# Routed attention and a cosine router with eight experts: an earlier transpose of the last batch's first logits, and one more GpSimd drain near the end

## The chip, the cores and the metric

The kernel runs on one NeuronCore of a Trainium2 chip. The metric is the device time of one execution in microseconds (us), as the median of several runs. TensorE is called PE here and in the profile, VectorE DVE, ScalarE ACT, GpSimd POOL and SyncE SP; SP issues most DMAs, and POOL those whose rows are picked by an index (gathers and scatters).

## The reference, cut to what matters

Attention comes first: 4 batches, 8 heads, 768 tokens, 64 wide. Queries and keys are assigned to the nearest of 16 centroids of their head, and a query attends only to the keys of its own cluster. The heads of a token, side by side, are a row x of 512 numbers. A router then picks one of 8 experts for every one of the 3072 rows, and the expert's two layers are applied:

```python
mask = q_assign[:, :, :, None] == k_assign[:, :, None, :]
attn = softmax(where(mask, q @ k.T / 8, -1e9));  x = rows(attn @ v)   # (3072, 512)
logits = unit(x) @ unit(expert_emb).T / tau                           # (3072, 8)
expert_idx = argmax(logits, axis=1)
gate_w = softmax(logits)[arange(N), expert_idx]
for e in range(8):
    mask = expert_idx == e
    out[mask] = gate_w[mask, None] * (relu(x[mask] @ w1[e]) @ w2[e])
```

## The kernel before, in words

Every engine executes its instructions in the order in which the program writes them: the whole kernel stands under a manual schedule for all five engines. What an instruction needs from another engine it waits for at its place, and what stands behind it on its own engine waits with it.

**Attention.** The loop over `units` goes through 16 pairs (a batch and two heads), each in two halves of the queries and six groups of keys. `scores` multiplies on PE, `expo` takes the exponential on ACT, `attend` multiplies with v on PE and lets DVE add up the weights in `acc`. For each half (`g`) `total` sums `acc` over the partitions with PE and takes the reciprocal on DVE (line 562), `divide` makes the finished x, turned, in `xT` (line 589, DVE), and `rows` turns it back on DVE (line 606) and stores it by DMA from SP in `x_rows` (line 613).

**Routing of a batch** (`route_pieces`). `products` multiplies `xT` with the experts' unit rows on PE into a bank of PSUM from `misc` (line 632); `misc` has two banks, taken in turns. `logits` is one transpose on DVE out of that bank into the tile `lt` (line 644). `read` loads the rows x again from `x_rows` for `norms`, which ACT takes. `choose` finds the best expert on DVE and counts on POOL. For the last batch the halves come apart: `products(0)` is issued in the last turn of the attention loop, directly behind that loop's last `rows`, and `products(1)` and `logits(1)` come after the last `divide`.

**Gates.** `gate_pieces(0, B - 1)` holds four steps for the first three batches: `gates[0]` a root on ACT, `gates[1]` three DVE instructions, `gates[2]` an exponential on ACT, `gates[3]` four DVE instructions (lines 710 to 716) and four small DMAs from SP to `gate_rows`.

**Experts.** `Places` computes for every token its place in the list of its expert. The rows of an expert are worked off in items. Four `early` items of 128 rows (`E0`) are filled from the first batches. Sixteen `later` items follow: eight `sized` ones of 272 down to 160 rows ("wide items"), and eight `block` ones of 128, by turns, the last being a block. An item has its expert's `w1` and `w2` loaded by SP into one of two slots (2 MB each), its rows fetched by gathers from POOL (`fetch`), turned (`turn_x`), multiplied with `w1` (`hidden`, line 1261, or `sized_hidden`, line 1176), passed through a relu on ACT, multiplied with `w2` (`result`, line 1277, or `sized_result`, line 1213), weighted by the gates and scattered to `out` by POOL (line 1052). `result` issues one scatter of 128 rows itself. A wide item's scatters, one for each 128 pieces of a quarter row, are issued by `send` one item later; the last wide item, of 160 rows, has five, and they come in the turn of the last block (`i == LAST`) ahead of its own `hidden`.

At the very end the framework adds (line 1633): SP waits for the semaphores of all DMAs, each engine executes a drain, and all engines meet at a barrier.

Of the kernel before, what the change touches and what calls it, by code (L numbers as in the profile page):

```python
# [39 lines left out]
def kernel(  # L40
# [12 lines left out]
    nc = tc.nc  # L53
# [637 lines left out]
    def gate_pieces(b0, b1):  # L691

        n = NJ * (b1 - b0)
        own = slice(NJ * b0, NJ * b1)
        lg, sq = lg_all[:, own], sq_all[:, own]

        def root():
            nc.scalar.activation(sq, sq, ACTF.Sqrt)

        def gate_scale():  # L700
            nc.vector.tensor_scalar(sq, sq, 1e-6, None, ALU.add)
            nc.vector.reciprocal(sq, sq)
            nc.vector.tensor_tensor(lg, lg, bc(sq, [P, n, E], 2), ALU.mult)

        def gate_exp():
            nc.scalar.activation(lg, lg, ACTF.Exp)

        def gate_sum():
            gate = gate_p[:, own]
            nc.vector.tensor_reduce(gate, lg, axis=AXX, op=ALU.add)  # L710
            nc.vector.tensor_scalar(gate, gate, 1e-9, None, ALU.add)
            nc.vector.reciprocal(gate, gate)

            if b0 > 0:
                return
            nc.vector.transpose(gate_t, gate_p)
            to = gate_rows[S * b0 : S * b1].rearrange("(j g t) o -> g j (t o)", g=NQ, t=SQ)
            for g in range(NQ):
                nc.sync.dma_start(out=to[g], in_=gate_t[SQ * g : SQ * g + n])

        return root, gate_scale, gate_exp, gate_sum
# [328 lines left out]
    def scatter(to, at, of, n):  # L1050

        inst = nc.gpsimd.indirect_dma_start(  # L1052
            out=to,
            out_offset=bass.IndirectOffsetOnAxis(ap=at, axis=0),
            in_=of,
            in_offset=None,
            bounds_check=n - 1,
            oob_is_err=False,
        ).ins
        tc.declare_no_dep(  # L1060
            inst, group="out", reason="a row of out is written by one slot of one item"
        )
        tc.add_to_no_dep_group("out", inst)
# [16 lines left out]
    def weights1(it, parts=1):  # L1080
        it.e = expert_of(it)
        for i in range(parts):
            load_part(w1s[it.slot], moe_w1, it.e, KD, i, parts)

    def weights2(it, parts=1):
        for i in range(parts):
            load_part(w2s[it.slot], moe_w2, it.e, KF, i, parts)
# [35 lines left out]
    def order_x(it):  # L1123

        d = mo[it]
        d["rows"] = xip.tile([P, KD, NQ, SQ], F32, tag="rows", name="rows")
        nc.gpsimd.tensor_copy(d["rows"], d["xin"].rearrange("p w (c i) -> p c w i", i=SQ))
# [29 lines left out]
    def order_w2(it):  # L1157

        w2 = mo[it]["w2"] = szp.tile([P, KF, DM], F32, tag="w2o", name="w2o", bufs=1)
        for f in range(KF):  # L1160
            nc.vector.tensor_copy(
                w2[:, f].rearrange("p (g w i) -> p g w i", w=NQ, i=SQ),
                w2s[it.slot][:, f].rearrange("p (w g i) -> p g w i", w=NQ, i=SQ),
            )
# [75 lines left out]
    def send(it):  # L1240

        u0 = FIRST[it.j]
        for u in range(WIDE[it.j]):
            at = flat(spidx)[:, u0 + u : u0 + u + 1]
            scatter(out_pieces, at, mo[it]["ys"][:, u], NQ * N)
        del mo[it]

    def flat(t):
        return t.rearrange("p k w -> p (k w)")

    def hidden(it, halves=(0, 1)):

        d = mo[it]
        for half in halves:
            if half == 0:
                d["hT"] = mop.tile([P, F], F32, tag="hT", name="hT")
            f0 = 512 * half
            bk = psH.tile([P, 512], F32, tag="h_ps", name="h_ps")
            for m in range(0, 512, P):
                for c in range(KD):  # L1260
                    nc.tensor.matmul(  # L1261
                        bk[:, m : m + P],
                        lhsT=w1s[it.slot][:, c, f0 + m : f0 + m + P],
                        rhs=d["xT"][:, P * c : P * c + P],
                        start=(c == 0),
                        stop=(c == KD - 1),
                    )
            nc.scalar.activation(d["hT"][:, f0 : f0 + 512], bk, ACTF.Relu)  # L1268
# [133 lines left out]
    with tc.manual_schedule(engines=by_hand):  # L1402
# [49 lines left out]
        products, logits, read, norms, choose = route[B - 1]  # L1452
        pb = Places(1, rtb)
        gates = gate_pieces(0, B - 1)
        gates[0]()
        hidden(E0[0], (0,))
        order_x(E0[3])
        total(ngroups - 1)
# [7 lines left out]
        hidden(E0[0], (1,))  # L1466
        gates[3]()
        weights1(E0[2])
        logits(0)
        read(0, NJ, P - SQ, P)  # L1470
        products(1)
        hidden(E0[1], (0,))
# [48 lines left out]
        def overflow():  # L1521
            n_used = nc.values_load(used[0:1, 0:1], min_val=0, max_val=KX + NO)
            slot = later[-1].slot

            def more(j0, n):
                for j in range(j0, j0 + n):
                    it = Item("whole", KX + j, slot, more_tables)
                    it.col, it.gates, it.xin = j, more_gates, xin
                    weights1(it)
                    weights2(it)  # L1530
                    fetch(it)
                    order_x(it)
                    turn_x(it, nc.scalar.copy)
                    hidden(it)
                    result(it)

            with tc.If(n_used > KX):  # L1537
                more_tables = [None] + [
                    mop.tile([P, NO], I32, tag=f"more{i}", name=f"more{i}", bufs=1)
                    for i in range(2)  # L1540
                ]
                xin = szp.tile([P, max(WIDE), P], F32, tag="ys", name="ys")[:, 0:NQ]
                pb.hot_blocks(NB, NO)
                pb.tokens(NO)
                pb.token_rows(more_tables[1], more_tables[2])
                more_gates = mop.tile([P, NO], F32, tag="more_gates", name="more_gates", bufs=1)
                pb.hot_gates(NO)
                pb.gates(more_gates)
                more(0, MORE[0])
                with tc.If(n_used > KX + MORE[0]):  # L1550
                    more(MORE[0], MORE[1])
                    with tc.If(n_used > KX + MORE[0] + MORE[1]):
                        more(MORE[0] + MORE[1], MORE[2])

        LAST = len(later) - 1
        for i, it in enumerate(later):
            if i == LAST - 1:
                overflow()
                weights1(later[LAST])
                weights2(later[LAST])  # L1560
            if it.kind == "sized":
                order_w2(it)
            if i + 1 < len(later):
                turn_x(later[i + 1])
            if i > 0 and i + 2 < len(later) and later[i + 2].kind == "sized":
                fetch(later[i + 2])
            if i > 0 and later[i - 1].kind == "sized":
                send(later[i - 1])
            if it.kind == "sized":
                sized_hidden(it)  # L1570
            else:
                hidden(it)
            if i == 0:
                pb.gates(slot_gates)
            for j in range(i + 2, min(i + 4, len(later))):
                if later[j].kind == "block" and later[j] not in mo:
                    if it.kind == "sized":
                        nc.gpsimd.tensor_copy(pace, mo[it]["hT"][0:1, KF - 1, 0:1])
                        fetch(later[j])
            if i + 2 < LAST:  # L1580
                weights1(later[i + 2])
                if it.kind == "sized":
                    weights2(later[i + 2])
            if it.kind == "sized":
                sized_result(it)
            else:
                result(it)
            if i == 0:
                fetch(later[2])
                spread_gates()  # L1590
            if i + 2 < LAST and it.kind != "sized":
                weights2(later[i + 2])
# [45 lines left out]
```

## Time and profile before

| | |
|---|---|
| time, median of 3 runs | 716.82 us (714.88 to 720.92) |
| own time of the profiled execution | 709.36 us |
| its span, first to last instruction | 707.6 us |
| granted PE clock, mean of the span | 0.995 |
| busy: PE, DVE, ACT, POOL | 690.8, 382.6, 265.1, 264.2 us |
| transpose of `logits` at 344.34, DVE | 0.24 us |
| gate arithmetic on DVE around it | 342.19 to 344.41 |
| the last wide item's scatters, POOL | 687.44 to 693.52 |
| the last block's scatter, POOL | 700.93 to 701.90 |
| closing drain of POOL | 6.02 us, from 700.7 |

A profile is one execution. Its times count from the first instruction. A row of a timeline gives start, duration, engine, line, operation, output and inputs, and in brackets the idle time of the engine before it with what ended that. PEld is the loading of weights into PE, which goes on beside the matmuls. An engine's name with a q (POOLq, SPq) is its instruction queue: drains, semaphore waits and the issuing of DMAs are counted there and not as busy time. In a table by stretches each row has the stretch, its length, the busy time and number of instructions of PE, PEld, DVE, ACT and POOL, then the granted PE clock (1.00 is full), the share of the DMA engines and GB/s.

### The profile page before, as it was taken

The page shows a single profiled execution, that of the slowest core. Times are in us where ns is not written, and L with a number is a line of the kernel's source. Part 1 is how long each engine was busy: PE and PEld are TensorE (multiplying, and loading weights), DVE is VectorE, ACT ScalarE, POOL GpSimd, SP SyncE. Part 2 cuts the span into 40 slices and gives each one's busy share as a digit, 9 for nine tenths or more (in the row PEclk, how much of TensorE's full clock was granted, in tenths as well). Part 3 has the DMA queues.
Part 4 walks back from the last instruction along what each step waited for, and adds up shares of the span by engine and source line. Part 5 has one row for each costly group of instructions (what it writes and reads, how often), then busy time and mean ns, then how long its engine had stood idle before and what let it go on. Part 6 is the DMA issues. An engine that isn't in the chain of part 4 may idle for free.

```text
span 707.6 us, 16122 instructions
## 1 busy us (share of the span) xinstructions
PE 690.8 (98%) x6518; PEld 456.2 (64%) x6518; DVE 382.6 (54%) x665; ACT 265.1 (37%) x446; POOL 264.2 (37%) x402
## 2 busy tenths in 40 slices
PE   6999999999999999999899999999999999999995
PEld 3444444444444444455876668897979797979793
DVE  4788888989889999989483121340220303031210
ACT  4566665677566755676215110101010111111110
POOL 2122222322224222353213546736264554544412
PEclk9999999999999999999999999999999999999999
DMA  9536665886657678879798987268668686869450
GB/s 150 91 60 110 105 104 87 153 159 108 100 108 146 120 146 152 183 190 329 184 278 305 342 314 268 81 233 287 258 226 299 198 310 226 320 242 330 142 192 28
DMA packets 244124, 135.55 MB, mean 192 GB/s; under 512 B 207808, under 2 KB 207810, under 8 KB 244044
## 3 DMA queue, kind: packets, MB, share of 16 engines
q1 hardware_dynamic: 237852, 121.28, 64.0%
q0 software_dynamic: 6016, 13.12, 5.4%
q8 instruction: 54, 0.88, 0.5%
q14 instruction: 26, 0.21, 0.1%
q10 hardware_dynamic: 176, 0.05, 0.0%
HBM read 115.92 MB, written 13.12 MB: 182 GB/s over the span
## 4 chain that ended last, share of the span: by engine, by line
PE 79%; DVE 6%; DMA 5%; issue 5%; POOL 1%; SPq 1%; ACT 1%; POOLq 0%; DVEq 0%; ACTq 0%
PE s_ps L484 18%; PE o_ps L506 15%; PE y_ps L1277 10%; PE h_ps L1261 9%; PE h_ps L1176 9%; PE y_ps L1213 5%; PE misc L1213 5%; DMA out_dram<-ys,spidx 3%; PE x_ps L1176 3%; DVE acc L525 2%; DMA x_rows<-xb 2%; PE misc L396 2%; PE misc L553 2%; PE misc L632 1%; SPq L613 1%
## 5 line engine op out<-in xcount | busy, mean ns | idle before, releaser
L495 ACT ACTIVATE prob<-s_ps 128x768 f32<-128x768 f32 x192 | 153.7, 812 | 95.2 <-PE s_ps L484 82.1
L484 PE MATMUL s_ps<-qT,kT 64*64 64x384 f32 x1536 | 156.0, 482 | 0.0
L506 PE MATMUL o_ps<-prob,v 64*64 64x385 f32 x1536 | 142.0, 486 | 0.0
L525 DVE TENSOR_TENSOR acc<-acc,prob 128x768 f32<-128x768 f32 x128 | 125.6, 982 | 8.8 <-ACT cd L422 0.5
L506 PEld LDWEIGHTS o_ps<-prob,v 64*64 64x64 f32 x1536 | 54.6, 133 | 70.3 <-issue 58.5
L1261 PE MATMUL h_ps<-xTm,w1s 128*128 128x128 f32 x768 | 90.0, 278 | 0.0
L1261 PEld LDWEIGHTS h_ps<-xTm,w1s 128*128 128x128 f32 x768 | 89.0, 195 | 1.4 <-issue 1.0
L1222 DVE STREAM_TRANSPOSE ys<-y_ps 128x256 f32<-128x256 f32 (+4 forms) x16 | 6.7, 417 | 153.4 <-PE y_ps L1213 153.4
L539 POOL TENSOR_TENSOR o_sum<-o_sb 128x385 f32<-128x385 f32 x30 | 32.0, 1067 | 146.3 <-ACT o_sb L530 146.3
L1052 POOL DMA_INDIRECT out_dram<-ys,spidx x56 | 56.7, 1013 | 74.7 <-DVE ys L1236 59.8
L1277 PE MATMUL y_ps<-w2s,hT 128*128 128x512 f32 x192 | 84.5, 593 | 0.0
L484 PEld LDWEIGHTS s_ps<-qT,kT 64*64 64x64 f32 x1536 | 56.0, 133 | 38.1 <-issue 34.9
L1176 PE MATMUL h_ps<-xTs,w1s 128*128 128x272 f32 (+7 forms) x384 | 72.9, 346 | 1.1 <-ACTq L1537 1.1
L1176 PEld LDWEIGHTS h_ps<-xTs,w1s 128*128 128x128 f32 x384 | 66.6, 190 | 8.0 <-issue 2.4
L1268 ACT ACTIVATE hT<-h_ps 128x512 f32<-128x512 f32 x24 | 14.3, 596 | 148.1 <-PE h_ps L1261 148.1
L484 PE MATMUL s_ps<-hot 64*64 64x384 bf16 x768 | 64.7, 325 | 2.2 <-ACT prob L495 1.1
L1041 POOL DMA_INDIRECT xs<-x_rows,gpidx x56 | 57.3, 1023 | 17.1 <-issue 16.8
L574 POOL COPY inv<-inv 32x12 f32<-32x12 f32 x120 | 43.0, 358 | 54.6 <-DVE inv L571 50.2
L1277 PEld LDWEIGHTS y_ps<-w2s,hT 128*128 128x128 f32 x192 | 35.6, 190 | 40.2 <-issue 40.2
L484 PEld LDWEIGHTS <-hot 64*64 64x64 bf16 x768 | 23.6, 106 | 39.4 <-issue 38.1
L1213 PE MATMUL y_ps<-hTs,w2o 128*128 128x272 f32 (+7 forms) x256 | 48.0, 346 | 0.0
L1213 PE MATMUL misc<-hTs,w2o 128*128 128x272 f32 (+7 forms) x256 | 48.0, 346 | 0.0
(264 smaller groups left out, 679.5 us busy)
## 6 DMA issues: line engine op xcount, KB each, us to landing
w1s<-in_moe_w_dram SPq DMA_DIRECT2D x18, 2048.0 KB, 10.6
w2s<-in_moe_w_dram SPq DMA_DIRECT2D x18, 2048.0 KB, 13.3
v<-in_v_dram SPq DMA_DIRECT2D x128, 48.0 KB, 2.1
q<-in_q_dram SPq DMA_DIRECT2D x60, 96.0 KB, 3.4
k<-in_k_dram SPq DMA_DIRECT2D x60, 96.0 KB, 3.6
x_rows<-xb SPq DMA_DIRECT2D x60, 96.0 KB, 2.8
xr<-x_rows SPq DMA_DIRECT2D x9, 512.0 KB, 4.0
w1s<-in_moe_w_dram SPq DMA_DIRECT2D x4, 1024.0 KB, 9.9
```

The lines of the kernel that those rows point to most:

```text
L484: nc.tensor.matmul(s_ps[D * half : D * half + D, h, 0:HS], lhsT=l[rows, half], rhs=r[rows], start=part == (1 if len(parts) < 2 else 0), st ...
L495: nc.scalar.activation(d["prob"][:, :, 0:HS], d["s_ps"][:, :, 0:HS], ACTF.Exp, scale=scale)
L506: nc.tensor.matmul(g["o_ps"][D * h : D * h + D, half, 0:HE], lhsT=ld[n]["v"][keys, j, h], rhs=d["prob"][keys, h, 0:HE], start=(j == 0), st ...
L525: nc.vector.tensor_tensor(g["acc"], g["acc"], d["prob"][:, :, 0:HS], ALU.add)
L539: add(t["o_sum"][:, hq], t["o_sb"][:, 0], t["o_sb"][:, 1], ALU.add)
L574: nc.gpsimd.tensor_copy(inv2[M * to : M * to + M, :, i % 2], inv[M * i : M * i + M])
L1041: nc.gpsimd.indirect_dma_start(out=to, out_offset=None, in_=of, in_offset=bass.IndirectOffsetOnAxis(ap=at, axis=0), bounds_check=n - 1, oo ...
L1052: inst = nc.gpsimd.indirect_dma_start(out=to, out_offset=bass.IndirectOffsetOnAxis(ap=at, axis=0), in_=of, in_offset=None, bounds_check=n - 1,
L1176: nc.tensor.matmul(bk, lhsT=w1s[it.slot][:, c, P * f : P * f + P], rhs=d["xT"][:, c, 0:C], start=(c == 0), stop=(c == KD - 1),)
L1213: nc.tensor.matmul(bks[g][:, 0:C], lhsT=d["w2"][:, f, P * g : P * g + P], rhs=d["hT"][:, f, 0:C], start=(f == 0), stop=(f == KF - 1),)
L1261: nc.tensor.matmul(bk[:, m : m + P], lhsT=w1s[it.slot][:, c, f0 + m : f0 + m + P], rhs=d["xT"][:, P * c : P * c + P], start=(c == 0), stop ...
L1277: nc.tensor.matmul(bk, lhsT=d["hT"][:, P * c : P * c + P], rhs=w2s[it.slot][:, c], start=(c == 0), stop=(c == KF - 1),)
```

## The change

The call `logits(0)`, the transpose of the first half of the last batch's logits, moves from behind `gates[3]` and the load of an expert's `w1` to directly behind `gates[0]`, ahead of the last half's `total`. In the turn of the last item, a drain instruction of POOL is added behind the scatters that `send` issues.

```diff
         pb = Places(1, rtb)
         gates = gate_pieces(0, B - 1)
         gates[0]()
+        logits(0)
         hidden(E0[0], (0,))
         order_x(E0[3])
         total(ngroups - 1)
...
         hidden(E0[0], (1,))
         gates[3]()
         weights1(E0[2])
-        logits(0)
         read(0, NJ, P - SQ, P)
         products(1)
         hidden(E0[1], (0,))
...
             if i > 0 and later[i - 1].kind == "sized":
                 send(later[i - 1])
+                if i == LAST:
+                    nc.gpsimd.drain()
             if it.kind == "sized":
                 sized_hidden(it)
```

## Prediction

> **What bounds the kernel now.** I read the page first, its busy rows and clock row, then the chain of work that ended last, then the timelines of the two stages that the diff touches.
>
> ```profile
> PE 690.8 (98%) x6518; PEld 456.2 (64%) x6518; DVE 382.6 (54%) x665; ACT 265.1 (37%) x446; POOL 264.2 (37%) x402
> PEclk9999999999999999999999999999999999999999
> ```
>
> TensorE (PE) is busy for 98% of the span, so there is little to win but in its few holes, in stretches where it is busy but slow, and in what lies behind its last matmul. The digits of PEclk are too coarse to show a short drop of the clock; a table by stretches is needed for that. The chain of waits around the end of attention (start, duration, what):
>
> ```profile
> 343.90 0.28 DVE gate_p L712
> 344.18 0.02 issue
> 344.20 0.21 DVE gate_t L716
> 344.41 0.18 DVE lt L644
> 344.59 0.04 issue
> 344.63 0.87 PE misc L632 x32
> 345.50 5.40 PE h_ps L1261 x32
> 350.90 0.44 PE x_ps L1152 x4
> 351.34 3.57 PE h_ps L1261 x32
> ```
>
> Two things stand here. The path runs over VectorE (DVE): `products(1)` (L632) waits for `logits(0)` (L644), which stands in DVE's order behind the gate arithmetic. And two equal halves of an expert, 32 matmuls each, take 5.40 and 3.57 us. From 355 us on the chain is PE without a hole up to the last item, but for the branch around 667 us. The timelines of PE and DVE say what else was ready:
>
> ```profile
> 332.96 0.87 PE L632 MATMUL misc<-xT,embT 128*32 128x96 f32 x32
> 338.81 3.74 PE L1261 MATMUL h_ps<-xTm,w1s 128*128 128x128 f32 x32
> 344.63 0.87 PE L632 MATMUL misc<-xT,embT 128*32 128x96 f32 x32 [2.08 <-DVE lt L644]
> ...
> 335.88 0.57 DVE L606 STREAM_TRANSPOSE xb<-xT 128x384 f32<-128x384 f32 x1
> 338.44 2.56 DVE L562 RECIPROCAL den<-misc 128x384 f32<-128x384 f32 x1 [1.99 <-PE misc L553]
> 341.03 0.62 DVE L589 SCALAR_TENSOR_TENSOR xT<-o_sum,den 128x384 f32<-128x384 f32 x1
> ```
>
> PE sits idle from 342.55 (338.81 + 3.74) to 344.63. What `logits(0)` reads was ready at 333.83, and the other input of `products(1)`, xT of L589, at 341.65. The clock by stretches (PEclk is the third column from the right):
>
> ```profile
> 342.41:345.82 3.41, 1.32 (x37) 1.04 (x36) 1.90 (x8) 0.81 (x2) 0.00 (x0) 1.00 0.40 59
> 345.82:349.24 3.42, 3.42 (x18) 3.42 (x18) 1.15 (x7) 0.00 (x0) 1.18 (x6) 0.50 0.36 82
> 349.24:352.65 3.41, 3.41 (x33) 3.41 (x32) 0.00 (x0) 1.07 (x2) 2.70 (x3) 1.00 1.01 390
> ```
>
> After a stretch of 3.41 us in which PE was busy for 1.32, the next 3.42 us were granted half the clock: 18 matmuls where the following stretch has 33. That is the 5.40.
>
> The end of the span: two rows of GpSimd's (POOL's) timeline, two of the last line, L1633 (duration min/median/max in ns, first and last start), and one of SyncE's waits (total, times, longest):
>
> ```profile
> 692.55 0.97 POOL L1052 DMA_INDIRECT out_dram<-ys,spidx  x1 [0.30 <-issue]
> 700.93 0.97 POOL L1052 DMA_INDIRECT out_dram<-y,sidx  x1 [7.41 <-ACT y L1288]
> ...
> L1633 SPq EVENT_SEMAPHORE  x13: 17/28/25632, 678.0 to 707.5; - x13
> L1633 POOLq DRAIN  x3: 40/113/6017, 700.7 to 707.3; - x3
> ...
> SPq L1633 <- PEq L1633: 3.1, 2, 2.6
> ```
>
> SyncE's long wait runs from 677.95 for 25.63 us, to 703.58: the landing of the last scatter. POOL's closing drain starts at 700.70 and takes 6.02 us, to 706.72, 3.14 us beyond that landing. SyncE has finished its own list at 704.32 and waits 2.6 us at the barrier; POOL is what comes last there.
>
> **Part A, the transpose of `logits(0)` moved forward.** It is one DVE instruction (L644, 0.24 us at 344.34) and no DMA. It is moved past DVE's reciprocal, divide, row transpose and seven gate instructions; no instruction of another queue changes place.
>
> At its new place it stands behind the row transpose that ends at 336.45. Its input has been ready for 2.6 us, so it waits for nothing. Queued behind it is the reciprocal (L562), for which DVE idles 1.99 us anyway, until PE's row sums at 338.4. The 0.24 us fall into that hole: cost nothing. If `products(0)` were later than 338.2, each us would hold the reciprocal, the divide and `products(1)`; it is 4.4 us away from that.
>
> At its old place it goes. `products(1)` then waits for xT (341.65) and for PE's own queue (342.55): PE is what is late next, so the whole hole of 2.08 us closes, less some 0.05 for the semaphore. The `misc` bank into which it writes was freed by `logits(0)` itself, at 336.7.
>
> With the hole goes the half clock. By the starts, L1261 of E0[1]'s first half took 350.74 - 345.43 = 5.31 us; its second half, at full clock, 354.75 - 351.17 = 3.58. That is 1.73 us more. Part A: 2.03 + 1.73 = **3.8 us**.
>
> [...]
>
> Does the 3.8 us survive? PE meets no wait from 355 to 650 us. Most weight loads are released by PE and move with it. One is not: w1 of E0[2], issued by SyncE at 346.90 behind the gate rows, lands at 355.0. PE wants it at 361.97, then at 358.2: 3.2 us of room. The gate gathers (first issue 349.34, median 5.3 us to landing) are in by about 356.5, the first of them by 355; the first eviction that reads one moves from 362.01 to 358.2. `choose` and the counts move forward about 1.2 us (DVE does `logits(1)` at 344.41 instead of 345.57) and the ranks on PE, then at 351.0, need them at about 347.5. The rank arithmetic on DVE (355.1 to 371.7) hangs on PE and shifts with it.
>
> **Part B, the drain behind the last wide item's five scatters.** Before it stand those scatters: the last issued at 692.55, landed some 2.2 us later (median of these issues in the last 22 us), at about 694.75. Behind it on POOL stands one thing, the last block's scatter, whose y is ready at 700.66. No other engine waits for POOL. So the cover is 5.9 us from that landing.
>
> The trace has no drain in mid-kernel. From below: a drain with nothing outstanding takes 0.04 to 0.11 us, by the same row. From above: the closing drain's remainder, 3.14 us beyond a landing. The latter is nearest, since scatters are outstanding here too: 694.75 + 3.14 = 697.9, hidden with 2.8 us to spare. [...]
>
> What it brings depends on what those 3.14 us are. The transfers of that stretch (703.58 to 706.72) are one packet:
>
> ```profile
> DMA packets 1, 0.01 MB, mean 3 GB/s; under 512 B 0, under 2 KB 0, under 8 KB 0
> q14 instruction: 1, 0.01, 0.7%
> ```
>
> No data move; 8 KB of instructions are fetched. Either the drain settles all transfers since the start of the kernel one by one, or it fetches code that 700 us of other work pushed out. In both cases an early drain pays in the idle 5.9 us, and the closing one has one scatter to settle: it ends near 703.58 + 0.5 at most. Then SyncE, at 704.32, is late next. Behind the barrier come 0.88 us (706.72 to 707.6), so the span would end at 705.2: 2.4 us less. The lower end is 0 (the 3.14 us are paid by each drain), the upper 2.4, since SyncE's list stays. I take **2.4**: drains with nothing to settle are short, so the cost is not that of any drain.
>
> **Sum.** 3.8 + 2.4 = 6.2 us. The profiled execution has a span of 707.6 and its own time of 709.36; they become 701.4 and 703.2. It lies 7.5 us under the median of the runs shown, and nothing in the change scales with that difference, so I take the 6.2 from the median: 716.82 - 6.2 = **710.6**.
>
> **Rivals.**
> - The closing drain stays as long as it was. For it: one remainder of 3.14 us is all that is known, and code fetched early may be pushed out by the scatter between. Against it: that is a single instruction. 716.82 - 3.8 = 713.0.
> - The gain of part A is eaten, because PE, 3.8 us earlier, meets something that has not moved, and only the drain pays: 716.82 - 2.4 = 714.4. Against it stand the margins above, 3.2 us at the least.
> - On the other side: the load of w1 for E0[2] takes longer beside gate gathers that now start 1.2 us earlier. It took 8.1 us (346.90 to 355.0); PE waits from 11.3 us on. A wait over 2 us would bring the half clock back, +1.73. From 13.4 us part A is gone; against part B it turns slower near 15.8 us, and at 17 us it is about 1.2 us slower: 718.0. The median landing is 10.6 us for w1 and 13.3 for w2, all under heavier traffic; that speaks against it.
> - The change not doing what it says: the order on all five engines is written by hand, so the moved line is moved. A drain that settles nothing is the first rival.
>
> **Chances.** Forecast (both parts, with or without the clock's share) 0.62; drain without effect 0.22; part A eaten 0.11; slower 0.05. The three runs shown spread by 0.84% of their median, so 1% is about what a measurement can tell from no change: 7.2 us, or 709.65. The forecast lies 1 us short of it; with an error of some 3 us in a median of such runs, it falls beyond in about four of ten of its cases, the first rival in one of ten: faster 0.3, slower by over 1% 0.04, within 1% 0.66. The range runs from the forecast less 4 (run error, upper cost) to the eaten case plus 1.6: 706.5 to 716.
>
> **What would show it.** Right: PE's wait on lt L644 is gone; no stretch under full clock between 340 and 355; both halves of E0[1] near 3.6 us; the closing POOL drain ends within 0.6 us of the last landing, and SyncE's wait at the barrier falls from 2.6 to under 0.3. Wrong: a new PE wait on w1s or misc before 365; a closing drain still 3 us beyond the landing; a last scatter issued over 1.2 us after its y is begun.

## The result, and the profile after

The changed kernel takes **709.1 us** (median of 6 runs, 707.91 to 710.36) where the kernel before took 716.14 beside it (6 runs, 713.96 to 720.92): a ratio of 0.9904, 95% interval 0.9885 to 0.9923. The forecast was 710.6, range 706.5 to 716.0. The gain, 0.96%, falls just inside "within 1%".

The profiled execution of after has a span of 707.4 us, against 707.6 before. That pair must not be compared: before's profile is of an execution 7 us below the median of its runs and is none of those runs; the experiments show where most of the 7 us can lie (under "two profiles side by side"). So I compare stages, each counted from an event that the change can't move: the last score matmul of attention, the ranks on PE (L768), the last matmul, the end of the span.

PE and then DVE of after, around the moved transpose (start, duration, engine, line, operation):

```profile
340.60 3.74 PE L1261 MATMUL h_ps<-xTm,w1s 128*128 128x128 f32 x32
344.27 0.87 PE L632 MATMUL misc<-xT,embT 128*32 128x96 f32 x32
345.06 3.84 PE L1261 MATMUL h_ps<-xTm,w1s 128*128 128x128 f32 x32
...
349.18 3.74 PE L1261 MATMUL h_ps<-xTm,w1s 128*128 128x128 f32 x32
352.75 0.25 PE L768 MATMUL misc<-cumx,onesb 128*128 128x200 bf16 x1
```

```profile
338.16 0.24 DVE L644 STREAM_TRANSPOSE lt<-misc 128x96 f32<-128x96 f32 x1
340.22 2.56 DVE L562 RECIPROCAL den<-misc 128x384 f32<-128x384 f32 x1 [1.82 <-PE misc L553]
```

`products(1)` (L632) has no bracket any more: it starts as E0[0]'s second half ends. The two halves of E0[1] last 3.84 and 3.74 us here, where the same view of before has 5.47 and 3.74. The transpose ends at 338.40, and DVE then still waits 1.82 us for PE's row sums: it is free, as costed. The clock (third column from the right) is full there:

```profile
344.00:349.00 5.00, 5.00 (x71) 4.74 (x70) 2.93 (x15) 0.87 (x3) 0.99 (x5) 1.00 0.30 45
```

From the last score matmul to `products(1)` it takes 13.27 us (15.42 before), to the ranks 21.75 (25.53 before). So in these two executions part A, the moved transpose, is 3.78 us: 2.15 of idle time and 1.63 of clock.

The end of the span: POOL's two rows with ACT's between them, the added drain at L1570, then the framework's line (L1635 now), and SyncE's waits:

```profile
694.76 0.97 POOL L1052 DMA_INDIRECT out_dram<-ys,spidx  x1 [0.30 <-issue]
...
702.19 0.69 ACT L1288 ACTIVATE y<-y_ps,slot_gates 128x512 f32<-128x512 f32 x1 [4.69 <-PE y_ps L1277]
703.15 0.97 POOL L1052 DMA_INDIRECT out_dram<-y,sidx  x1 [7.42 <-ACT y L1288]
```

```profile
L1570 POOLq DRAIN  x1: 8878/8878/8878, 691.6 to 691.6; - x1
```

```profile
L1635 POOLq DRAIN  x3: 46/113/2956, 702.9 to 707.1; - x3
```

```profile
SPq L1635 <- DMA out_dram<-y,sidx: 26.9, 1, 26.9
...
SPq L1635 <- PEq L1635: 0.3, 1, 0.3
```

The added drain enters the queue at 691.58, while the five scatters are still being issued, and ends at 700.46. POOL is idle from 695.73 to 703.15, and the y of the last scatter is ready at 702.88 (702.19 + 0.69): the drain fits with 2.42 us to spare. The closing drain falls from 6.02 to 2.96 us. It ends at 705.88, 0.08 beyond the landing of the last scatter; before it was 3.14 beyond. SyncE's wait at the barrier falls from 2.6 to 0.3. From the last matmul to the end of the span: 8.22 before, 5.83 now.

### The profile page after: what moved, and what is told of

Read it like the earlier page. It is cut to its first block, busy times and chain, and to the rows that moved or that the text cites. A ratio compares the mean times of both kernels' runs of the same rounds, so it can differ in the third digit from the quotient of the medians.

```text
span 707.4 us, 16123 instructions
## 1 busy us (share of the span) xinstructions
PE 692.3 (98%) x6518; PEld 455.4 (64%) x6518; DVE 382.0 (54%) x665; ACT 264.5 (37%) x446; POOL 263.0 (37%) x402
## 4 chain that ended last, share of the span: by engine, by line
PE 80%; DVE 6%; issue 5%; DMA 5%; another core or an unknown queue 1%; ACT 1%; POOL 1%; SPq 1%; POOLq 0%; DVEq 0%; ACTq 0%
PE s_ps L484 19%; PE o_ps L506 15%; PE h_ps L1261 10%; PE y_ps L1277 9%; PE h_ps L1176 9%; PE y_ps L1213 5%; PE misc L1213 5%; PE x_ps L1176 3%; DMA out_dram<-ys,spidx 3%; DVE acc L525 2%; PE misc L553 2%; PE misc L396 2%; DMA x_rows<-xb 1%; PE misc L632 1%
```

## The experiments

Runs of one group share a chip. Landings here are the semaphore events that the DMAs raise, and a "remainder" is the time from the last landing to the end of a drain.

**First group: each part alone, both, and the hole filled.** Before: 712.44 us.

`e1_move_only` is the diff without the drain; `e2_drain_only` is the diff without the move; `e4_both` is the changed kernel. `e3_fill_hole` is the kernel before with work for the idle PE, and changes nothing else:

```diff
         read(0, NJ, P - SQ, P)
+        fill_ps = psH.tile([P, 512], F32, tag="h_ps", name="h_ps")
+        for _ in range(9):
+            nc.tensor.matmul(fill_ps.rearrange("p (g x) -> p g x", x=P),
+                lhsT=onesb, rhs=bc(onesb, [P, 4, P], 1), start=True, stop=True)
         products(1)
```

> Only the transpose of the first logits is moved; no drain is added. The theory (the move is worth the hole of 2.08 us and the 1.7 us of half clock behind it): 3.8 us faster than before; in the profile no PE wait on lt L644, no half clock between 340 and 355 us, both halves of E0[1] near 3.6 us, and POOL's closing drain still some 3 us beyond the last landing. Rival (the clock drop is not the hole's doing): 2.1 us faster, and a stretch of half clock near 345 us stays. Rival (the gain is the drain's alone): no change.

> Only the drain behind the last wide item's scatters is added; the logits stay where they were. The theory (the closing drain settles what the early one has already settled): 2.4 us faster; from the landing of the last scatter to the end of the span 1.6 us instead of 4.0, while the hole of some 2 us before products(1) and the half clock stay. Rival (every drain costs its 3 us): no change, the closing drain still 3 us beyond the landing. Rival (the early drain holds the last scatter): the last scatter starts more than 1.2 us after its eviction began, and the time is level or slower.

> The kernel before, with nine idle matmuls (bf16, 128x512, some 0.22 us each, results unused) ahead of products(1), in PE's hole of 2.08 us; nothing is moved and no drain is added. The hole stays as a wait in the order of the work, but PE is busy in it. The theory (the half clock is the answer to the hole): no half clock behind it, E0[1]'s first half takes 3.6 us instead of 5.3, and the time falls by 1.5 to 1.7 us while products(1) starts as late as before. Rival (the slow stretch has another cause, for instance the weights and rows that land at that time): it stays slow, no change in time.

> The changed kernel again, beside its two parts on one chip. The theory (two independent terms): 6.2 us faster than before, the sum of the two parts run alone (3.8 and 2.4). Rival (the parts overlap): less than the sum.

| kernel | median, us | ratio to before, 95% | mean against before, us | last score matmul to `products(1)` | last score matmul to ranks | last matmul to end |
|---|---|---|---|---|---|---|
| before | 712.44 | | | 15.42 | 25.53 | 8.22 |
| e1 move only | 709.19 | 0.9958 (0.9942 to 0.9974) | -3.1 | 13.27 | 21.75 | 8.22 |
| e2 drain only | 709.94 | 0.9964 (0.9950 to 0.9979) | -2.6 | 15.42 | 25.53 | 5.82 |
| e3 hole filled | 712.59 | 1.0001 (0.9988 to 1.0015) | 0.0 | 15.42 | 23.91 | 8.22 |
| e4 both | 706.14 | 0.9914 (0.9896 to 0.9932) | -6.2 | 13.27 | 21.75 | 5.82 |

(The stages of before are those of the profile shown at the start; the standard error of each difference of means is about 0.4 us.) The parts add up within that error: 3.1 + 2.6 = 5.7 against 6.2. Neither needs the other. The move alone gave 3.1 where 3.8 had been expected. The closing drain of e1 and that of e2:

```profile
L1633 POOLq DRAIN  x3: 40/113/6015, 700.6 to 707.1; - x3
```

```profile
L1635 POOLq DRAIN  x3: 46/113/2945, 703.7 to 707.9; - x3
```

With the move alone it stays at 6.02; with the drain alone it is 2.95. In e2 the hole stays and so does what follows it:

```profile
342.78:346.19 3.41, 1.33 (x37) 0.99 (x36) 1.86 (x10) 0.81 (x2) 0.00 (x0) 1.00 0.77 112
346.19:349.60 3.41, 3.41 (x18) 3.41 (x18) 1.30 (x7) 0.00 (x0) 1.20 (x6) 0.50 0.26 53
```

In e3 PE is busy through the hole, on matmuls that nobody reads, and the clock holds: 3.84 us for the first half of E0[1].

```profile
343.32 2.11 PE L1473 MATMUL h_ps<-onesb 128*128 128x512 bf16 x9
345.57 0.87 PE L632 MATMUL misc<-xT,embT 128*32 128x96 f32 x32
346.37 3.84 PE L1261 MATMUL h_ps<-xTm,w1s 128*128 128x128 f32 x32
```

So the half clock followed from the idle time, and it is worth 25.53 - 23.91 = 1.62 us in a profile (that e3 kept the clock by chance is excluded further down, with e13). Yet over 12 runs e3 gains nothing, where 1.5 to 1.7 us had been expected. Either the drop does not happen in most executions of before, or something takes the gain back.

**Second group: what the drain pays for, and the hole once more.** Before: 715.24 us.

`e5_three_drains` drains POOL in three turns:

```diff
-                if i == LAST:
+                if i in (3, 9, LAST):
                     nc.gpsimd.drain()
```

> The changed kernel with two more drains, behind the scatters sent in the turns 3 and 9 of the sixteen later items. What is in dispute is what a drain of GpSimd pays for beyond the landing of its last transfer: 3.15 us closed the kernel before (164 gathers and scatters), 3.47 us the added drain (163), 0.08 us the closing one behind it (1). Theory of settling one by one, some 0.02 us each: the drain in turn 3 (about 67 transfers so far) some 1.3 us beyond its last landing, the one in turn 9 and the one in the last turn (some 45 to 50 new ones each) near 1.0. Rival, a fixed price of a drain that has been away for long: 3.1 to 3.5 us each. Rival, code that is fetched once: 3.1 to 3.5 in turn 3 and next to nothing after that.

One run, 710.63 us. The three added drains:

```profile
L1570 POOLq DRAIN  x3: 7387/13697/15002, 477.0 to 693.0; - x3
```

They end 2.78, 2.37 and 1.98 us beyond their last landings, with 67, 57 and 39 transfers of POOL since the start or the drain before; the closing one, with one transfer, 0.08. In the changed kernel the last of these drains has 163 transfers behind it and a remainder of 3.47. So a remainder is not a price of every drain, and not code fetched once and then kept: it comes again, smaller where fewer transfers are new. About 0.04 us a transfer was my estimate (2.78 / 67 and 2.37 / 57), and I took it that the 163 pay less than 163 shares because older ones were settled on the way, which no trace shows. (The times of the landings are the last ones on record: in this group's traces about half of these records are missing.)

`e8_move_and_idle` is the changed kernel with e3's nine matmuls ahead of `products(1)`: the move, but PE's time given back. `e9_fill_again` is e3 once more. `e7_warm_start` goes after the half clock that the opening of after's profile shows from 15.99 to 19.40 us, with more of the kernel's own idle matmuls:

```diff
         piece(0, "choose")
-        keep_up(6)
+        keep_up(10)
         piece(0, "turn_numbers")
+        keep_up(4)
```

> The changed kernel with the nine idle matmuls ahead of products(1), where there is no hole any more. Filling the hole of the kernel before gave full clock and 1.6 us back by the ranks, but no time on the whole. Theory A (the added matmuls cost only their own 2.1 us, and the fill's 1.6 us were lost by chance or in a part of the executions that never had the drop): 4.1 us under before, 2.1 over the changed kernel. Theory B (18 more instructions on PE make its later stalls, the waits that the profile puts down to issue, longer by some 1.5 us): 2.5 us under before, 3.6 over the changed kernel.

> The hole filled with nine idle matmuls a second time, for another profile of it: from the last score matmul to the ranks 23.9 us again (25.5 in the kernel before), full clock behind products(1). Open is the stretch from the ranks to the last matmul: 344.6 us in the profile before, 346.3 to 348.8 in the others. Theory B (the added instructions lengthen it): 348 us or more again. Theory A (chance): anywhere from 344.6 to 348.8.

> The changed kernel with eight more idle matmuls in the opening: ten instead of six ahead of the turning of the first numbers, and four behind it, in two holes of some 1.0 us each at 13 and 15 us. In two of five profiles so far a stretch of half clock followed these holes (from 16 to 19.4 us), and it cost some 1.8 us there. Theory (holes of about 2 us in all within one 3.41 us stretch bring the half clock, wherever they lie): no half clock at 16 us, and 0.5 to 1 us faster than the changed kernel on average, so 6.7 to 7.2 us under the kernel before. Rival (the opening's drop is harmless or has another cause): the same as the changed kernel, 6.2 us under before, or a stretch of half clock in spite of them.

e8: 711.72, ratio 0.9950 (0.9934 to 0.9966), 3.6 us under before by the means. The drain's 2.4 are in that; the idle time is given back but for 0.21 (15.21 to `products(1)`); about 1 us is left for the clock, less than its 1.63. e9: 715.62 in one run, no gain to be seen either, and in this execution 23.91 to the ranks. e7: 710.07, ratio 0.9925 (0.9905 to 0.9946). Its profile has full clock up to the last matmul, and yet attention ends at 330.89 us, where it ended at 331.00 with the drop and at 330.04 in e4, which had none: the added matmuls cost about what the drop did. The gain that was expected of them did not come.

**Third group: a drain in another place.** Before: 709.59 us. The changed kernel with `if i == 9` and with `if i == 3` in place of `if i == LAST`.

> The changed kernel with its POOL drain in the turn of i == 9 in place of the last one: some 124 POOL transfers stand before it, and 40 behind it up to the end. Theory A (a drain pays 0.0415 us for each transfer not yet settled, without limit): the mid-kernel drain ends 5.1 us beyond the last landing, the closing drain 1.7 us beyond its own, so that the last matmul to the end of the span is some 6.7 us (5.83 in the changed kernel, 8.22 before). Theory B (the same price, but no more than some 75 transfers are ever open to be settled): 3.1 to 3.5 us beyond the landing at i == 9, and again 1.7 us at the end. Rival C (only how long ago the last drain was matters): 3.1 or more in both places.

> The changed kernel with its POOL drain in the turn of i == 3: 67 POOL transfers before it, 97 behind it. All theories: the mid-kernel drain ends 2.8 us beyond the last landing, as it did with three drains. Theory A (0.0415 us for each transfer, without limit): the closing drain ends 4.0 us beyond the last landing, and the last matmul stands 9.1 us before the end of the span. Theory B (never more than some 75): 3.1 us and 8.2, as without any added drain.

One run each: e10 704.04 us, e11 **710.71**, 1.1 above the single run of before; the stages below say more than that pair can. The closing drains, e10 and then e11:

```profile
L1635 POOLq DRAIN  x3: 46/113/4542, 696.8 to 702.0; - x3
```

```profile
L1635 POOLq DRAIN  x3: 46/113/9202, 698.8 to 708.6; - x3
```

From the last matmul to the end of the span e10 takes 6.75 us and e11 11.41, where before took 8.22. With 40 transfers since its last drain, e10's closing remainder is 1.68, as every theory with 0.04 us a transfer had it. The rest went against all of them. With 97 transfers e11's closing remainder is 6.34, and so longer than the 3.15 of a kernel that never drained before and has 164 behind it. And e10's drain at `i == 9`, with 124 transfers, has only some 0.8.

One account, my own estimate worked out afterwards from these drains, fits every long drain of these traces to 0.1 us; no run was made to test it. By it a drain goes twice through the transfers that are still open, at about 0.0415 us each: the first time while the last of them land, the second time behind that. Where the landing is early, the drain ends both passes after the last scatter's row on POOL, whose end in e11 is 700.06:

```profile
699.08 0.98 POOL L1052 DMA_INDIRECT out_dram<-y,sidx  x1 [7.43 <-ACT y L1288]
```

The drain ends at 708.05, 7.99 us later, and 2 x 0.0415 x 97 = 8.05. For e10's 40 it is 3.33, with 3.32 by the sum. Where the landing is late, the second pass alone stands behind it: 0.0415 x 67 = 2.78, as measured at `i == 3` in e5 and in e11. A kernel that reaches 164 without a drain pays for 58 (4.81 us measured and reckoned, the closing drain of before), at 163 for 57 (4.73, the added drain of after), and at 124 for about 18 (0.75; 0.78 measured). In all three, 106 are no longer open. So by this account the open transfers are counted from the start or the last drain, and the count starts anew after about 106; e11's drain at 67 put that off, and the 97 behind it were all still open at the end. Why 106, and where those were settled, no trace here shows.

**Two profiles side by side.** Before: 709.62 us on this chip. The changed kernel and the kernel before, both with a profile.

> The changed kernel once more, beside the next run. Theory A (the changed stage and the end of the span are all that the change touches; the holes of PE put down to issue near 400, 559, 631 and 665 us come with the chip or the execution, not with the change): last score matmul to products(1) 13.27 us, to the ranks 21.75, last matmul to the end of the span 5.83, as in every execution with both parts, and the ranks to the last matmul the same as in the next run to 1 us if both run without these holes (344.6 us where there were none); time 5.5 to 6.5 us under the kernel before. Rival B (the earlier PE brings the holes with it): the holes are here and not in the next run, ranks to the last matmul 346.5 to 349.6, time 2.5 to 5 us under.

> The kernel before, for a second profile of it on the chip of the run above. Theory A: 15.42 us from the last score matmul to products(1), 25.53 to the ranks if the half clock follows the hole and 23.9 if not, 8.22 from the last matmul to the end; the ranks to the last matmul as in the run above, to 1 us if neither has the holes. Rival B: 344.6 here whatever the run above shows.

e12: 704.94, ratio 0.9924 (0.9907 to 0.9940), 4.7 us under before, less than the 5.5 to 6.5 expected; its stages are those expected, 13.27, 21.75 and 5.82. e13: 707.88 in its one run. This pair answers two open points.

First, where before's low profile came from. On PE the first two groups, and the profile of after, show pauses of 0.2 to 1.8 us. Most have no releaser in the trace ("issue"; near 400, 559 and 597 us), others stand behind a late relu of ACT (near 631 and 665 us in after). The first two rows are after; the third is e12 at the same place, the fourth e13's stretch of 5 us there, with PE busy for all of it (second number):

```profile
400.67 0.27 PE L1261 MATMUL h_ps<-xTm,w1s 128*128 128x128 f32 x1 [0.29 <-issue]
402.08 3.17 PE L1261 MATMUL h_ps<-xTm,w1s 128*128 128x128 f32 x27 [1.14 <-issue]
```

```profile
398.79 5.08 PE L1261 MATMUL h_ps<-xTm,w1s 128*128 128x128 f32 x44
```

```profile
400.00:405.00 5.00, 5.00 (x61) 4.88 (x61) 1.21 (x4) 1.19 (x2) 0.46 (x1) 1.00 1.02 354
```

From the ranks to the last matmul, e10, e11, e12 and e13 all take 344.59 or 344.60 us, as before's first profile did; the other nine take 346.26 to 349.65, with and without the move alike. It is the group, not the change, that decides: before is at 709.6 us where the pauses are missing and at 712 to 716 where they are. What they wait for the trace doesn't say. One thing goes with them in all fourteen profiles: the nine with pauses hold only about half of the landing events of POOL's transfers (1239 of 2624 in after), the five without hold nearly all (2613 in e12). So a releaser can be missing from the record, and whether the pauses and the lost records have one cause is open.

Second, when the clock drops. e13 has the same hole of 2.08 us, and no drop: 23.90 us to the ranks.

```profile
344.78 0.87 PE L632 MATMUL misc<-xT,embT 128*32 128x96 f32 x32 [2.08 <-DVE lt L644]
345.57 3.84 PE L1261 MATMUL h_ps<-xTm,w1s 128*128 128x128 f32 x32
```

The clock changes of all traces lie on a grid of 3.413 us whose place in the span differs from execution to execution. In before's first profile the clock changes at 345.82, 349.24 and 704.22 us, 1 and 104 steps of the grid apart; in after's at 15.99, 19.40 and 705.48, 1 and 201 steps apart. Counted back from e13's own change at 701.39, its windows are these:

```profile
339.58:342.99 3.41, 3.12 (x28) 2.93 (x27) 3.27 (x6) 1.45 (x2) 0.00 (x0) 1.00 1.10 174
342.99:346.40 3.41, 1.62 (x39) 1.48 (x40) 1.86 (x9) 0.81 (x2) 0.00 (x0) 1.00 0.41 60
346.40:349.81 3.41, 3.41 (x33) 3.41 (x33) 0.79 (x5) 0.36 (x1) 1.51 (x7) 1.00 0.43 120
```

The border at 342.99 cuts the hole: 0.29 us of it lie in the first window, 1.79 in the second, and the clock stays full. In before's first profile and in e2 the whole hole lay in one window, 2.08 us idle, and the next was granted half. The opening of e12 narrows the point of the drop: PE is 1.41 us busy in a window, so 2.00 idle, and half the clock in the next.

```profile
14.30:17.71 3.41, 1.41 (x24) 1.09 (x28) 1.92 (x10) 1.89 (x5) 0.00 (x0) 1.00 1.57 141
17.71:21.12 3.41, 3.41 (x28) 1.88 (x31) 2.79 (x4) 1.41 (x3) 0.00 (x0) 0.50 1.24 126
```

The same stretch of the opening lies differently in the grid in each of the thirteen executions without e7's added matmuls: the six in which its emptiest window is 1.51 to 1.75 us idle kept the clock, the seven with 2.0 to 2.1 lost it. So a window of these traces with 1.79 us idle kept the clock and one with 2.00 lost it; at the end of e4 and e11, windows 1.89 and 1.87 us idle (from 697.95 and 696.54) still kept it. In e3 and e9 the place of the hole lies wholly in one window (343.02 to 346.43 and 344.12 to 347.53, counted back from their changes at 704.84 and 709.34): what kept the clock there were the idle matmuls.

For a hole of 2.08 us that falls anywhere in the grid, some window holds 1.89 or more of it in (3.41 - 2.08 + 2 x 0.19) / 3.41 = 50% of executions and 2.00 or more in (1.33 + 2 x 0.08) / 3.41 = 44%. The clock's part of A is then a little under half of 1.63, 0.7 to 0.8 us on the mean, as an estimate from these rows. The mean granted clocks of the first group's runs point the same way but can't decide: they make 1.8 us less at half clock in e1 than in before and 0.8 less in e3, each with an error of some 0.9, where a drop in half the executions would make 1.7.

With it most of the means fall into place: move 2.15 + 0.8 = 2.95 (e1: 3.1), drain 2.4 (e2: 2.6), both 5.35 (e12 against the eight runs of before in its group: 709.5 - 704.6 = 4.9), move with idle matmuls 2.4 + 0.2 + 0.8 = 3.4 (e8: 3.6). Two are some two standard errors off: e4, where 5.35 is due and 6.2 came, and e3, where 0.8 is due and 0.0 came; whether e3's nine matmuls cost something later was not settled.

## Why the prediction was right

**The chain of reasons held.** `products(1)` waited for a transpose that stood behind other work on DVE, and PE's own queue is what is late next: the idle time gone is 2.15 us in each of the profiles with the move (taken: 2.08 less 0.05), but for e8, which fills the time again. The transpose at its new place costs nothing: DVE waits 1.82 us for PE behind it (predicted 1.99 less 0.24, so 1.75). No new wait appears on w1s or misc before 365 us. That the load for E0[2] or the gate gathers would eat the gain is refuted up to the ranks, where the full 3.78 us are seen, and beyond them by e12 and e13, which take the same 344.60 us from there to the last matmul; the slower rival, w1 landing late, did not come.

**The clock's share was over-sized.** In the profile it is 1.63 us, near the 1.73 taken. But the step that charged it in every execution failed: e13 has the hole and no drop. The prediction took it from the row of one profile. For one execution that was right, a hole of 2.08 us did bring the drop in the first profile and in e2; for a median it was half right. In e2 one window held all 2.08 us of the hole, in e13 1.79 of them: 3.8 should have been 2.15 plus a share of 1.6, some 3.0 by the estimate above.

**The drain was sized right, for a reason only half understood.** 2.4 us taken, 2.4 in the last stage of every profile that has the drain in the last turn, 2.6 in the runs of e2. SyncE is late next, as named. The cover was as costed: the five scatters land at 697.0, 2.2 us after the last is issued, and y is ready 5.9 us later. Only the remainder was a little short, 3.47 and not 3.14, so that 2.42 us were to spare and not 2.8. Of the two causes named, settling of earlier transfers and a fetch of code, e5 and e11 exclude code that is fetched once: a drain that ran earlier in the same kernel did not make a later one cheap. And beside the added drain of after (691.58 to 700.46) no instruction packet moves, where the closing one of before had one of 8 KB. Settling is the reading that remains, though no trace shows it at work. But "all transfers since the start" is not what is settled: 164 cost no more than 58 would by the price of the other drains. That an early drain must leave the closing one cheap held only because the drain stands directly ahead of the last scatter; e11's made it dearer.

**The sum.** Predicted 6.2; the medians gave 7.0 (the result), 6.3 (e4) and 4.7 (e12), and the stages with the clock's mean share 5.35. So the mechanism was right and the sum too high by some 0.8; that it stands in the middle of the measured gains is in part luck, since the result's own gain is 1.7 above what the stages account for. The forecast of 710.6 lies 1.5 us above the result, part of it the base: the before beside the result had 716.14, not 716.82. On the chip without pauses the sum from the profiled execution, 703.2, met e12's best execution, 703.3 at full clock up to the end; its other three took 704.7 to 705.3.

## What to carry to other kernels

A transpose or copy that a busy engine waits for belongs where its input is ready and its own engine waits anyway (here DVE, for 1.82 us); look up what stands in front of it in its queue. Count a hole in PE at its length, and the half clock behind it by the chance that one clock window holds nearly all of it (of these windows of 3.413 us, one with 2.00 us idle lost the clock and one with 1.89 kept it), not as certain because one profile shows it. If the closing drain of GpSimd outlasts the last landing (here by 3.14 us), drain once in idle time just ahead of the last transfer (2.4 us less at the end here), and look at the closing drain again: a drain long before it saved less in one place (e10, 1.47 us) and made the end longer in another (e11, by 3.19).

## What the runs showed of the hardware that was not expected

- The half clock falls on a grid of 3.413 us whose place differs from execution to execution: 2.00 us idle in one window lost the clock for the next, 1.89 kept it.
- A GpSimd drain in mid-kernel took 7.4 to 15.0 us, 0.8 to 3.5 of them beyond the last landing. A drain at `i == 3` lengthened the closing one from 6.02 to 9.20 us. All of them fit the estimate of two passes at about 0.0415 us for each open transfer, counted anew after some 106; passes and count are fitted, not tested.
- The same program differs by 3 to 6.5 us from group to group. Pauses of PE, 1.7 to 5.1 us of them in a profile, go with the slower groups; where they are missing, a stretch of 344.6 us repeats to 0.01 us. The traces with pauses have lost half of the landing events of POOL's transfers.
